# An attention kernel's start and end rearranged: loads in single blocks, statistics and paddings moved between engines, one key block in halves, another end of the exponential stream

## The chip, the cores and the metric

The kernel runs on one core of one Trainium2 chip. Its time is the device time of one execution in microseconds (us). The span in a profile, first to last instruction, is some 1.8 us shorter (867.1 in the profiled run of the kernel before, which took 868.85). Names of the engines: PE multiplies matrices (TensorE), PEld loads its weights, ACT is ScalarE, DVE is VectorE, POOL is GpSimd, SP issues DMA transfers. All runs gave correct results.

Ratios are the mean time of one kernel's fast runs over the mean of the other's fast runs of the same rounds on the same chip. So a ratio is not quite the ratio of the medians quoted beside it.

## The reference, cut to what matters

```
xn = layernorm(x)                                  # x: 2048 x 640
qkv = xn @ wqkv                                    # 32 heads of 20 columns
scores = einsum("bhqd,bhkd->bhqk", q, k) * 20**-0.5
p = softmax(scores);  o = einsum("bhqk,bhkd->bhqd", p, v);  s = o @ wo
g = silu(B(xn))        # a second branch: layernorm, two products over 2048 and 1536, gelu
out = x + s * g
```

The exponentials of the softmax are the bulk: 32 x 2048 x 2048 of them. ACT takes most in pieces of 128x1024 scores ("doubles", two banks of PSUM); DVE computes the rest with an integer formula in units of 128x512, so two DVE units equal one ACT double. They sum to 2,048 halves, for instance 888 doubles, one single and 271 units.

## The kernel before

The program is written by a builder in Python: a list scheduler with a model of durations decides the order of each engine's instructions. The parts that the change touches:

```python
    DMA_LAT = 1900.0                  # the scheduler's model of a load
    DMA_RATE = 300.0
    ACT_STATS = (1, 5)                # blocks of x whose mean and variance ScalarE computes
    DVE_TAIL_GUARD = 3                # DVE takes no unit among the last 3 of a pass
    # ... (cut)
        dma_x(0, 1)                   # block, number of blocks in one transfer
        dma_x(1, 1)
        dma_x(2, 1)
        dma_x(3, 1)
        dma_w(640, 736, wqk3[:, :, 640:736], S_("wk0"))      # first head group's weights
        dma_w(0, 96, wqk3[:, :, 0:96], S_("wq0"))
        dma_x(4, 4)
        dma_w(1280, 1440, wv_sb[:, :, 0:160], S_("wv0"))
        dma_x(8, 4)
        dma_x(12, 4)
    # ... (cut)
        add_job("wp0", [wp_step("dve", 1, 0, 250.0), wp_step("dve", 0, 0, 250.0), ("tag", "wpG0")], ("ln_s0",), 20.5)
    # ... (cut: the emission of one exponential on ScalarE)
            tk = pr.act(lambda e: e.activation(outp, inp, AF.Exp, ...),
                        reads=[bank_slot[b] for b in banks[:n]], writes=[...], name=f"exp{us[0]}", cost=...)
    # ... (cut: which unit DVE takes next)
            u = nxt[0]
            if u < NU and u + len(dg) > pass_end[u] - self.DVE_TAIL_GUARD:
                u = pass_end[u]
    # ... (cut: the last two output blocks; BA holds 512 columns, BB 128)
        BA, BB = (5, 0), (4, 1)
        def tail_fin(i):
            b = LBS[i]
            steps = op_mms(b, ps(BA[i]), 0, 512, bank_slot[BA[i]], False, True)
            steps += op_mms(b, ps(BB[i], 128), 512, 128, bank_slot[BB[i]], False, True)
```

Keys come in four blocks of 512 rows. A block of keys needs four 128-row blocks of x: statistics, normalization (DVE, with one POOL step), transposes (PE), an eviction, the projection (PE), another eviction.

The softmax here doesn't subtract the row's maximum and nothing guards it: scores larger than these inputs give would overflow.

Of the kernel before, what the change touches and what calls it, by code (L numbers as in the profile page):

```python
# [87 lines left out]
class Prog:  # L88
# [7 lines left out]
    DMA_LAT = 1900.0  # L96
    DMA_RATE = 300.0
# [185 lines left out]
class _Kern:  # L283
# [20 lines left out]
    ACT_STATS = (1, 5)  # L304
    H_PRIO = 88.0
    DVE_EXP = True
    DVE_TAIL_GUARD = 3
    NTMP = 4
# [90 lines left out]
    def schedule(self):  # L399
# [79 lines left out]
        dma_x(3, 1)  # L479
        dma_w(640, 736, wqk3[:, :, 640:736], S_("wk0"))  # L480
        dma_w(0, 96, wqk3[:, :, 0:96], S_("wq0"))
        dma_x(4, 4)
# [72 lines left out]
        def stat_steps(gb):  # L555
            steps = []
            b0 = gb * 4
            nm = f"ln{gb}"
            for b in range(b0, b0 + 4):
# [11 lines left out]
            steps.append(("tag", f"ln_s{gb}"))  # L571
            return steps

        def ln_steps(gb):
            steps = []
            b0 = gb * 4
            nm = f"ln{gb}"
            mvs = [S_(f"mv{b}") for b in range(b0, b0 + 4)]
            sr = S_(f"rstd{gb}")
            sw = S_(f"lnw{gb}")  # L580
            steps.append(("dve", lambda e: e.tensor_scalar(st(4, b0, 4), st(1, b0, 4), self.EPS, None, ALU.add), mvs,
                          [sw], f"{nm}ve", 100.0))
            steps.append(("pool", lambda e: e.tensor_tensor(st(2, b0, 4), st(4, b0, 4), mhalf(4), ALU.pow),
                          [sw, S_("mhalf")], [sr], f"{nm}pow", 1050.0))
            for b in range(b0, b0 + 4):
                steps.append(("dve", lambda e, b=b: e.tensor_scalar(xn_ap(b), regA[:, b, :], st_sb[:, 0, b:b + 1],
                                                                    st_sb[:, 2, b:b + 1], mean_op(b), ALU.mult),
                              [S_(f"x{b}"), mvs[b - b0], sr], [S_(f"xn{b % FC}")], f"{nm}ap", 360.0))
                steps.append(("tag", f"xn_b{b}"))
            steps.append(("tag", f"xn_g{gb}"))  # L590
            return steps

        def hstat_steps():

            mvs = [S_(f"mv{b}") for b in range(NB)]
            rs = [S_(f"rstd{gb}") for gb in range(4)]
# [22 lines left out]
        def wp_step(eng, w, G0, cost):  # L619
            dstp = bass.AP(wqk0_sb, w * 128, [[5 * 256, P], [256, 5], [32, GH], [1, 32]])  # L620
            srcp = bass.AP(wqk_sb, w * 640, [[6400, P], [1280, 5], [20, GH], [1, 32]])
            return (eng, lambda e: e.tensor_copy(dstp, srcp), [S_("wk0" if w else "wq0")], [S_(f"wp{w}_{G0}")],
                    f"wp{w}_{G0}", cost)
# [21 lines left out]
        def xT0_steps(half, dcs, nm):  # L645

            def make(bk):
                steps = []
                pb = ps_all[:, bk * 512:(bk + 1) * 512].bitcast(bf)
                for b in (2 * half, 2 * half + 1):  # L650
                    for i, dc in enumerate(dcs):
# [3 lines left out]
                            [S_(f"xn{b}"), S_("idb")], [bank_slot[bk]], "xT0", 128))  # L655
                n = len(dcs)
                dst = xnT_sb[:, dcs[0]:dcs[0] + n, half * 256:(half + 1) * 256]
                src = pb[:, 0:n * 256].rearrange("p (c n) -> p c n", c=n)
                steps.append(("ev", dst, src, "copy", None, [bank_slot[bk]], [S_(f"xT{dc}_0{half}") for dc in dcs],
                              "xTe0", n * 256))  # L660
                steps.append(("tag", f"xT0_{nm}"))
# [3 lines left out]
        def xsl(dc, tb, half=None):  # L665

            if tb:
                return [S_(f"xT{dc}_{tb}")]
            return [S_(f"xT{dc}_0{h_}") for h_ in ((0, 1) if half is None else (half,))]

        def qk0_steps(w, c0, n, half, nm):

            def make(bk):
                steps = []
                rd = [S_(f"wp{w}_0")] + [x for dc in range(5) for x in xsl(dc, 0, half)]
                for dc in range(5):
                    steps.append(("pe", lambda e, dc=dc: e.matmul(
                        ps(bk, n), wqk0_sb[:, dc, w, :], xnT_sb[:, dc, c0:c0 + n], start=(dc == 0),
                        stop=(dc == 4)), rd, [bank_slot[bk]], f"qk0_{w}_0{nm}", n))
                steps.append(("ev", qk_sb[:, 0, w, c0:c0 + n], ps(bk, n), "k" if w else "q", None,  # L680
                              [bank_slot[bk], S_("cq")], [S_(f"qkb0_{w}_0_{g}{nm}") for g in range(GH)], f"qke0_{w}_0{nm}", n))
                steps.append(("tag", f"qk0_{w}_0{nm}"))
# [3 lines left out]
        def qk_slots(slot, w, tb, g):  # L686
            if slot == 0 and tb == 0:
                return [S_(f"qkb0_{w}_0_{g}a"), S_(f"qkb0_{w}_0_{g}b")]
# [52 lines left out]
        def v_steps(b, half):  # L741
            def make(bk):
# [3 lines left out]
                for i, bb in enumerate(bl):  # L746
                    rd = [S_("wv0" if half == 0 else "wv")] + [x for dc in range(5) for x in xsl(dc, bb // 4, None if bb > 3 else bb // 2)]
# [328 lines left out]
        def unit_ok(u):  # L1076
            G, p, c, g = units[u]
            if G == 0 and c == 0 and p == 0:
                return "qk0_1_0a" in done and "qk0_0_0" in done
            return all(f"qk{G}_1_{x[0] // 4}" in done for x in parts[u]) and f"qk{G}_0_{p}" in done  # L1080

        def emit_st(lst, banks):
# [8 lines left out]
            for j2, (k2, i) in enumerate(rows_):  # L1091
# [11 lines left out]
                      reads=qk_slots(slot, 0, p, g) + (qk_slots(slot, 1, c // 4, g) if slot or c // 4 else  # L1103
                                                      [S_(f"qkb0_1_0_{g}" + ("a" if c == 0 else "b"))]), writes=[bank_slot[bk]],
# [192 lines left out]
        XT0 = ("a", "b", "c", "d", "e")  # L1297
        add_job("consts2", lambda bk: cst2 + [("tag", "qpad")], ("xn_g3",), 60.0)
        for gb in range(4):
            add_job(f"stat{gb}", stat_steps(gb), () if gb == 0 else (f"ln_s{gb - 1}",), 20.8 + gb)  # L1300
            rq = (f"ln_s{gb}",) + (() if gb < 3 else tuple(f"xT0_{d}" for d in XT0))
            add_job(f"ln{gb}", ln_steps(gb), rq, 20.0 + gb)
        for b in self.ACT_STATS:
            add_job(f"astat{b}", act_stats(b), (), 21.0 + b)
        add_job("wp0", [wp_step("dve", 1, 0, 250.0), wp_step("dve", 0, 0, 250.0), ("tag", "wpG0")], ("ln_s0",),
                20.5)
# [9 lines left out]
        def xts(b):  # L1316
            if b < 4:
                return tuple(f"xT0_{d}" for d in XT0)
            return tuple(f"xT{b // 4}_{d}" for d in (0, 2, 4))

        for nm, half, dcs in (("a", 0, (0, 1, 2, 3)), ("b", 0, (4,)), ("c", 1, (0, 1)), ("d", 1, (2, 3)), ("e", 1, (4,))):
            add_bank_job(f"xT0_{nm}", xT0_steps(half, dcs, nm), (f"xn_b{2 * half + 1}",), 22.0)
# [463 lines left out]
```

## Time and profile before

| | before |
|---|---|
| time, median of 3 runs | 870.96 us (868.67 to 871.2) |
| profiled run: time, span | 868.85 us, 867.1 us |
| first exponential starts | 15.16 |
| 27th exponential starts | 46.64 |
| last exponential ends (called E below) | 856.40 |
| end of the span | E + 10.70 |

The prediction shows the page's first lines, four stretches and the two timelines. Two more rows of the table of stretches cut the run at the 27th exponential (columns: stretch, length, busy us of PE, PEld, DVE, ACT, POOL with the number of instructions, clock, DMA share, GB/s):

```profile
15.16:46.64 31.48, 29.32 (x250) 15.26 (x253) 27.34 (x76) 27.61 (x32) 7.11 (x8) 1.00 0.34 81
46.64:856.40 809.76, 754.36 (x5470) 234.81 (x5555) 775.20 (x1911) 808.64 (x878) 0.00 (x0) 1.00 0.18 39
```

In the second row ACT is busy 808.64 of 809.76 us. The first one is the ramp. The chain that ended last shows the end of the run (start, length, engine and line):

```profile
859.41 0.33 PE ps_all L1216 x4
859.74 2.20 PE ps_all L873 x11
861.94 0.34 PE ps_all L878
```

L1216 are the last products of probabilities and values, L873 the eleven output products, L878 the closing ones that need the last rows of attention. DVE's epilogue makes these rows ready: it divides by the sums of the softmax and transposes, into a buffer called the stage.

### The profile page before, as it was taken

To read this page: it belongs to the slowest core of one execution; us is meant where nothing else is said; L and a number is where in the kernel's file an instruction comes from. 1 tells how busy PE (TensorE), PEld (TensorE's weight loads), DVE (VectorE), ACT (ScalarE), POOL (GpSimd) and SP (SyncE) were. 2 spreads that over 40 slices of the span, in tenths; PEclk is the share of its full clock that TensorE was granted. 3 is DMA by queue.
4 is the path that set the end of the run, shared out by engine and by line. 5 is a ranking of instruction groups with operands and counts; after the bars stand their busy time and mean duration, and the time that the engine had idled before them with its cause. 6 is when DMAs were issued, how large, how long until landed. Compare 5 with 4: busy or idle time off the path is not lost.

```text
span 867.1 us, 16589 instructions
## 1 busy us (share of the span) xinstructions
PE 801.2 (92%) x5837; PEld 260.4 (30%) x5928; DVE 820.6 (95%) x2040; ACT 844.8 (97%) x925; POOL 13.8 (2%) x22
## 2 busy tenths in 40 slices
PE   8999999999999999999899999999999999999997
PEld 4432222222232233322222322322222222222233
DVE  8989999999999999999999999999999999999998
ACT  6899999999999999999999999999999999999995
POOL 3200000000000000000000000000000000000000
PEclk9999999999999999999999999999999999999999
DMA  8141010011203113100013112122312200032120
GB/s 240 44 112 31 6 37 10 16 30 35 58 13 76 38 18 82 54 11 10 10 25 77 38 36 52 26 52 65 72 26 50 47 11 6 8 106 65 42 47 32
DMA packets 123303, 39.33 MB, mean 45 GB/s; under 512 B 84264, under 2 KB 122104, under 8 KB 123224
## 3 DMA queue, kind: packets, MB, share of 16 engines
q1 hardware_dynamic: 123224, 38.27, 18.9%
q8 instruction: 50, 0.82, 0.4%
q14 instruction: 29, 0.24, 0.1%
HBM read 25.88 MB, written 9.83 MB: 41 GB/s over the span
## 4 chain that ended last, share of the span: by engine, by line
ACT 82%; PE 10%; DVE 6%; issue 1%; DMA 1%; SPq 0%; DVEq 0%; ACTq 0%
ACT pt_sb L1129 80%; PE ps_all L1101 4%; DVE ew_sb L1169 1%; PE ps_all L1216 1%; DVE dpt_sb L1175 1%; PE ps_all L749 1%; ACT zt_sb L837 1%; DVE el_sb L1173 1%; PE ps_all L873 1%; DVE el_sb L1174 1%; DMA regA<-in_A_x_dram 1%; ACT zt_sb L832 1%; PE ps_all L804 1%; PE ps_all L697 1%; DVE el_sb L1171 0%
## 5 line engine op out<-in xcount | busy, mean ns | idle before, releaser
L1129 ACT ACTIVATE pt_sb<-ps_all 128x1024 bf16<-128x1024 f32 x889 | 820.3, 1136 | 3.1 <-PE ps_all L1101 2.1
L1101 PE MATMUL ps_all<-qk_sb 32*128 32x512 bf16 (+1 forms) x2112 | 367.5, 377 | 51.1 <-ACT pt_sb L1129 41.2
L1169 DVE TENSOR_SCALAR ew_sb<-ps_all 128x512 uint16<-128x512 uint16 x271 | 182.8, 685 | 26.9 <-PE ps_all L1101 25.2
L1101 PEld LDWEIGHTS ps_all<-qk_sb 32*128 32x128 bf16 x2112 | 97.6, 91 | 345.6 <-ACT pt_sb L1129 298.2
L1175 DVE SCALAR_TENSOR_TENSOR dpt_sb<-ps_all,el_sb 128x512 uint16<-128x512 f32 x271 | 179.7, 684 | 1.4
L1216 PE MATMUL ps_all<-pt_sb,v_sb 128*32 128x512 bf16 (+1 forms) x1832 | 162.7, 378 | 0.3 <-DVE dpt_sb L1175 0.3
L1173 DVE TENSOR_TENSOR el_sb<-ev_sb,el_sb 128x512 bf16<-128x512 bf16 x271 | 109.2, 417 | 0.5
L1174 DVE TENSOR_TENSOR el_sb<-el_sb,ew_sb 128x512 bf16<-128x512 bf16 x271 | 108.7, 418 | 0.4
L1216 PE MATMUL ps_all<-dpt_sb,v_sb 128*32 128x512 bf16 (+1 forms) x280 | 81.7, 378 | 0.3 <-DVE dpt_sb L1175 0.3
L804 PE MATMUL ps_all<-regB,regA 128*128 128x128 bf16 (+1 forms) x371 | 75.8, 300 | 1.4 <-issue 0.8
L1170 DVE TENSOR_SCALAR ev_sb<-ew_sb 128x512 bf16<-128x512 uint16 x271 | 74.1, 286 | 2.2
L804 PE MATMUL ps_all<-regC,regA 128*128 128x128 bf16 (+1 forms) x371 | 73.2, 300 | 1.3 <-issue 0.8
L1171 DVE TENSOR_SCALAR el_sb<-ew_sb 128x512 bf16<-128x512 uint16 x271 | 74.0, 285 | 0.0
L716 PE MATMUL ps_all<-xnT_sb,wqk_sb 128*112 128x512 bf16 x200 | 66.4, 403 | 0.3 <-DVE el_sb L1174 0.2
L1216 PEld LDWEIGHTS ps_all<-pt_sb,v_sb 128*32 128x32 bf16 x1832 | 36.0, 94 | 55.6 <-issue 49.0
L1682 PE MATMUL ps_all<-wrm_sb 128*128 128x512 bf16 (+1 forms) x145 | 44.8, 392 | 3.8 <-DVE ps_all L508 2.2
L804 PEld LDWEIGHTS ps_all<-regB,regA 128*128 128x128 bf16 x384 | 25.3, 97 | 40.1 <-issue 25.9
L804 PEld LDWEIGHTS ps_all<-regC,regA 128*128 128x128 bf16 x384 | 25.3, 97 | 38.5 <-issue 29.8
L749 PE MATMUL ps_all<-wv_sb,xnT_sb 128*128 128x160 bf16 (+1 forms) x160 | 33.7, 302 | 0.1
L873 PE MATMUL ps_all<-wo_sb,xnT_sb 128*128 128x128 bf16 (+2 forms) x154 | 30.9, 300 | 0.5 <-issue 0.3
L716 PEld LDWEIGHTS ps_all<-xnT_sb,wqk_sb 128*112 128x112 bf16 x200 | 21.4, 128 | 29.6 <-issue 10.8
L1690 PE MATMUL ps_all<-wrm_sb,v_sb 128*128 128x512 bf16 x80 | 28.4, 385 | 0.5 <-DVE rden_sb L1272 0.2
(89 smaller groups left out, 354.1 us busy)
## 6 DMA issues: line engine op xcount, KB each, us to landing
regA<-in_B_w_dram SPq DMA_DIRECT2D x6, 1024.0 KB
regA<-in_B_w_dram SPq DMA_DIRECT2D x8, 768.0 KB
regA<-in_A_x_dram SPq DMA_DIRECT2D x7, 640.0 KB
qkT_scratch_dram<-pk_sb SPq DMA_DIRECT2D x40, 112.0 KB
qk_sb<-qkT_scratch_dram SPq DMA_DIRECT2D x56, 80.0 KB
on_scratch_dram<-on_sb SPq DMA_DIRECT2D x124, 20.0 KB
out_dram<-regC SPq DMA_DIRECT2D x3, 640.0 KB
wqk_sb<-in_A_wqkv_dram SPq DMA_DIRECT2D x2, 680.0 KB
```

The source lines that it names most:

```text
L716: steps.append(("pe", lambda e, dc=dc: e.matmul(ps_all[0:112, bk * 512:(bk + 1) * 512], wqk_sb[:, dc * 1280 + c0:dc * 1280 + c0 + 112], xn ...
L804: steps.append(("pe", lambda e, k=k: e.matmul(ps(bk, n), wap[:, k, col0:col0 + 128], rows[:, k, c0:c0 + n], start=(k == 0), stop=(k == nk ...
L1101: pr.pe(lambda e, outp=outp, lhsT=lhsT, rhs=rhs, g=g: e.matmul(outp, lhsT, rhs, start=True, stop=True, tile_position=(32 * g, 0)), reads=q ...
L1129: tk = pr.act(lambda e: e.activation(outp, inp, AF.Exp, bias=-self.OFFS * math.log(2.0) / 128.0, scale=math.log(2.0) / 128.0), reads=[bank ...
L1169: (lambda e: e.tensor_scalar(w3, lo, 0x7FFF, None, ALU.bitwise_and), bs, [sw], dv(N)),
L1170: (lambda e: e.tensor_scalar(v_, w_, 1.0 / 256.0, -128.0, ALU.mult, ALU.add), [sw], [sv], dv(N, .26)),
L1171: (lambda e: e.tensor_scalar(l_, w_, a3 / 65536.0, (b3 - 64.0 * a3) / 256.0, ALU.mult, ALU.add), [sw], [sl_], dv(N, .26)),
L1173: (lambda e: e.tensor_tensor(l_, v_, l_, ALU.mult), [sv, sl_], [sl_], dv(N, .52)),
L1174: (lambda e: e.tensor_tensor(l_, l_, w_, ALU.mult), [sl_, sw], [sl_], dv(N, .52)),
L1175: (lambda e: e.scalar_tensor_tensor(o_, zr, -(self.OFFS - 16256.0), l_, ALU.add, ALU.add), bs + [sl_], [S_(f"dpt{s0 + i}") for i in range( ...
L1216: pr.pe(lambda e, outp=outp, lhsT=lhsT, rhs=rhs, k=k, g=g: e.matmul(outp, lhsT, rhs, start=(k == 0), stop=(k == NB - 1), tile_position=(0, ...
L1682: pe_full(lambda e: e.matmul(ps(wb, n), wrm_sb[:, 0:P], wrm_sb[:, P:P + n], start=True, stop=True), [S_("warm"), S_("warm1")], [bank_slot[ ...
```

## The change

The intent: start the exponentials earlier, close the hole in ACT's stream at key block 1, and shorten the end. The diff, cut to its core:

```diff
-    DMA_LAT = 1900.0
-    DMA_RATE = 300.0
+    DMA_LAT = 2000.0
+    DMA_RATE = 220.0
-    ACT_STATS = (1, 5)
+    ACT_STATS = (1,)
+    LN_GROUPS = ((0, 4), (4, 2), (6, 2), (8, 4), (12, 4))     # normalization: blocks 4-5 and 6-7 in pairs
+    LAST_GUARD = 10
@@ loads
+        dma_x(4, 1)
         dma_w(640, 736, ...)
         dma_w(0, 96, ...)
-        dma_x(4, 4)
+        for b in range(5, 8):
+            dma_x(b, 1)
@@ padding of the first head group's weights
-        add_job("wp0", [wp_step("dve", 1, 0, 250.0), wp_step("dve", 0, 0, 250.0), ...], ("ln_s0",), 20.5)
+        add_job("wp0", [wp_step(w) for w in (1, 0)] + [("tag", "wpG0")], (), 50.5)      # now on ScalarE
@@ key block 1 in halves
+            if gb == 1:
+                for nm, half, dcs in (("a", 0, (0, 1)), ("b", 0, (2, 3, 4)), ("c", 1, (0, 1)), ("d", 1, (2, 3)), ("e", 1, (4,))):
+                    add_bank_job(f"xT1_{nm}", xT0_steps(1, half, dcs, nm), ...)
+                    if nm == "b":
+                        add_bank_job("k0_1a", qk0_steps(1, 1, 0, 256, 0, "a"), ...)
+                add_bank_job("k0_1b", qk0_steps(1, 1, 256, 256, 1, "b"), ...)
@@ priority of probability-value products: later while the ramp lasts
-                    pr_ = 1.0 if nav >= self.PV_HI else (8.0 if ... else 70.0)
+                    pr_ = 1.0 if nav >= self.PV_HI else 30.0 if ramp[0] else (8.0 if ... else 70.0)
@@ the end
-        BA, BB = (5, 0), (4, 1)
+        BA, BB = (5, 7), (4, 0)
-            if u < NU and u + len(dg) > pass_end[u] - self.DVE_TAIL_GUARD:
+            if u < NU and u + len(dg) > pass_end[u] - (self.DVE_TAIL_GUARD if pass_end[u] < NU else self.LAST_GUARD):
+            if e == "dve" and nxt[0] >= NU:          # after the last unit, prefer DVE work of high priority that is ready soon
+                soon = [max(x[1], pr.T[e]) for x in cs_by[e] if x[0] <= 12.0]
+                if soon and min(soon) <= r + 130.0:
+                    r = min(soon)
```

## The prediction

> **What bounds the kernel now.** I read the page first (shares, forty slices, chain), then the timeline of ScalarE (ACT) at both ends, then the busy time of every engine in four stretches, then the waits.
>
> ```profile
> PE 801.2 (92%) x5837; PEld 260.4 (30%) x5928; DVE 820.6 (95%) x2040; ACT 844.8 (97%) x925; POOL 13.8 (2%) x22
> ...
> ACT 82%; PE 10%; DVE 6%; issue 1%; DMA 1%; SPq 0%; DVEq 0%; ACTq 0%
> ...
> L1129 ACT ACTIVATE pt_sb<-ps_all 128x1024 bf16<-128x1024 f32 x889 | 820.3, 1136 | 3.1 <-PE ps_all L1101 2.1
> ```
>
> ACT carries the end: 889 exponentials, with 3.1 us of idle in front of them in the whole run. Four stretches (columns: stretch, its length, then busy us of PE, PEld, DVE, ACT, POOL, clock, DMA share, GB/s) show where it is not busy:
>
> ```profile
> 0.00:15.16 15.16, 11.45 (x76) 7.70 (x76) 11.32 (x39) 7.50 (x15) 6.71 (x14) 1.00 0.90 277
> 15.16:44.81 29.65, 27.49 (x232) 14.29 (x234) 27.34 (x76) 25.79 (x29) 7.11 (x8) 1.00 0.30 68
> 44.81:856.40 811.59, 756.19 (x5488) 235.77 (x5573) 775.20 (x1911) 810.47 (x879) 0.00 (x0) 1.00 0.18 40
> 856.40:867.10 10.70, 6.03 (x50) 2.67 (x48) 6.76 (x17) 1.04 (x4) 0.00 (x0) 0.90 0.18 62
> ```
>
> So 811.6 us of 867.1 are a stream that ACT keeps full. Only the 15.2 us before the first exponential, the holes in the next 29.7 us, and the 10.7 us after the last one can shrink. ACT's timeline there:
>
> ```profile
> 9.81 0.74 ACT L549 ACTIVATE regC<-regA 128x640 bf16<-128x640 bf16 x1 [4.29 <-DMA regA<-in_A_x_dram]
> 10.45 0.19 ACT L549 ACTIVATION_READ_ACCUMULATOR regC<-regA 128x1 f32 x1
> 10.54 1.49 ACT L1023 ACTIVATE xnT_sb<-ps_all 128x1024 bf16<-128x1024 bf16 x2
> ...
> 15.16 7.72 ACT L1129 ACTIVATE pt_sb<-ps_all 128x1024 bf16<-128x1024 f32 x8
> 22.76 1.03 ACT L1023 ACTIVATE xnT_sb<-ps_all 128x1024 bf16<-128x1024 bf16 x1
> 25.22 0.78 ACT L1030 ACTIVATE qk_sb<-ps_all,cst_sb 128x512 bf16<-128x512 f32 x1 [1.42 <-PE ps_all L697]
> 26.48 3.90 ACT L1129 ACTIVATE pt_sb<-ps_all 128x1024 bf16<-128x1024 f32 x4 [0.48 <-PE ps_all L1101]
> ```
>
> The reader is to see two things. ACT waits until 9.81 for an x block that only feeds statistics, and the first transposed-x eviction stands behind it until 10.54. After eight exponentials (key block 0) the stream stops from 22.76 to 26.48 for key block 1: 3.7 us. Two smaller holes follow, 34.30 to 35.83 (key block 2) and 44.03 to 44.81 (key block 3), with one value eviction of 0.77 between.
>
> **What the Trainium skill says.** "TensorE: Matmul & The Clock Gate", Architectural detail, calls the ACT and DVE queues strict FIFO: an instruction that waits holds up those behind it. The trace agrees: the eviction at 10.54 waited behind the load. "ScalarE: Activation LUTs", What ACT_TABLE_LOAD costs, gives 186 ns + 0.833 ns per column for a plain activation, 719 ns for 640 columns; the trace has 737 ns for 128x640. That is my price for a weight padding on ACT. "DMA: Bandwidth & Descriptors", Specifications, puts the minimum for line rate at 512 B; the first weight loads have rows of 192 B, and the trace shows 162 GB/s from 5 to 6 us against 294 from 2 to 3 us. "Perfetto Trace Analysis", Engine Utilization, says at least one engine should approach full use in a well-tuned kernel; ACT at 97% does.
>
> **The change part by part.** Times are of the trace before; the order of instructions is that of the built program.
>
> *To the first exponential.* Statistics of block 5 leave ACT for DVE, so ACT no longer waits until 9.81. The two paddings leave DVE (0.30 and 0.35 us) for ACT, 0.74 each, in a gap of ACT that runs from 5.5 to about 9.8. The weights are now one 160 KB block later: they were there by 6.89 and 7.17; at 294 GB/s a block is 0.56 us, so by about 7.5 and 7.7, and the paddings end by 9.0 at worst. DVE now runs one half of block 4's statistics (0.36) ahead of the variance step, in place of one padding (0.22): x-normalization starts at 8.55 instead of 8.41. Block 4 should have landed: 820 KB are moved by 4.95, and block 2's semaphore came 1.2 us after its bytes, giving 6.2, before 6.89. The transposes of blocks 0 and 1 were done at about 9.75 before, so 9.9 now; the eviction starts then and not at 10.54. PE followed 1.15 us after it (11.69), so 11.05 now, and the rest of the chain is the same 2.9 us of projections and a last eviction. First exponential 15.16 - 0.6 = 14.55. **Gain 0.6 us.**
>
> *Key block 1.* Its blocks are normalized in pairs and transposed in halves, DVE takes these evictions. In the new order ACT runs 11 exponentials, one value eviction, 5 more: all 16 of key blocks 0 and 1 with no hole. Exponential 9 needs the first half by about 21.3; DVE, walked row by row, has it at 19.5. Exponential 13 needs the second by 25.1; DVE has it at 24.3, little room. The hole of 3.7 us closes.
>
> *What is given back.* DVE gets some 1.1 us of extra copies, 1.1 of key evictions and 1.1 of statistics, and loses 0.65 of padding and 0.96 of first evictions. Blocks 8 to 11 are normalized by about 28.2 instead of 26.15. Exponential 16 ends at 14.55 + 16*0.965 + 0.57 = 30.6. Then ACT has query block 1 (0.78), a transposed-x piece (0.57), a wait for five 512-column matmuls (1.24), key block 2 (0.78) and 0.5 for the score matmuls: exponential 17 at 34.5, 35.83 before. Key block 3's eviction also moves to ACT: 0.78 + 0.5 instead of 0.78 in all, and one value eviction follows (0.5). Exponential 25 at 43.5 (44.81 before), exponential 26 at 44.9 (45.75 before). **Of 3.7 us some 0.9 stay, the first part's 0.6 included.**
>
> *Middle.* 888 double exponentials in both; the last single one (707 ns) becomes a 272nd DVE unit. **Gain 0.5 us** at the spacing of the stream.
>
> *Tail.* Let E be the end of the last exponential, 856.40 before. The chain before, in DVE's timeline:
>
> ```profile
> 856.99 1.28 DVE L1175 SCALAR_TENSOR_TENSOR dpt_sb<-ps_all,el_sb 128x512 uint16<-128x512 f32 x2
> ...
> 859.78 0.45 DVE L1253 STREAM_TRANSPOSE tr_sb<-ps_all 128x256 f32<-128x256 f32 x1 [0.22 <-PE ps_all L1216]
> 860.26 0.20 DVE L1256 RECIPROCAL rden_sb<-tr_sb 128x8 f32<-128x8 f32 x1
> 860.50 0.33 DVE L1257 TENSOR_TENSOR on_sb<-tr_sb,rden_sb 128x160 bf16<-128x160 f32 x1
> 860.87 0.45 DVE L1258 STREAM_TRANSPOSE stage_sb<-on_sb 128x256 bf16<-128x256 bf16 x1
> 862.30 0.69 DVE L1455 TENSOR_TENSOR regC<-ps_all,regC 128x512 bf16<-128x512 f32 x1 [0.99 <-PE ps_all L878]
> ```
>
> DVE's last units end at E+1.9, the epilogue starts at E+3.4, its stage is ready at E+4.9, the last DVE operation ends at 864.58 = E+8.2, the output lands 2.5 later: E+10.7. With the guard of 10 units the last five exponentials leave DVE free: its last unit ends about E-2.6. The last probability-value matmuls wait for PE's five 512-column output matmuls and start at E+0.3, the epilogue at E+0.9, the stage is ready at E+2.4. But the second last block now takes bank 7, which three earlier jobs use in turn, so PE has 22 matmuls of 128 columns (0.1 each, to E+2.8), the first closing matmuls, then five of 512 columns (1.2) *behind* the stage, and two closing ones: E+4.8. ACT's evictions (0.8) and the last two DVE operations (1.0) follow, E+6.7, and the output at E+9.2. **Gain 1.5 us**, where the epilogue alone is 2.5 earlier.
>
> Sum: 0.9 + 0.5 + 1.5 = 2.9 us, 0.33%. From the median 870.96: 868.0.
>
> **The rivals.** (1) *The whole ramp gain stays*: if DVE is faster than my walk and key block 2 is ready when exponential 16 ends, 2 us more, 866. Against: four evictions on ACT in one place, and PE's order puts the transposes behind score matmuls. (2) *A new head-of-line wait takes the gain back*: ACT for the later weights, or DVE for block 4. The loads saturate the queues (DMA share 0.90 until 15 us); weights later than 9.8 would cost as much as the wait removed: 869 to 870. (3) *The DVE is the bound of the stream and the guard moves work the wrong way*: DVE is busy 95%, but it sat 25.2 us idle for score matmuls (L1169's row), so it has room; ACT's 3.1 us against it. (4) *The tail is bound by PE rather than by exponentials*: then only part of the 1.5 comes, 869. If bank 7 comes free sooner than I think, up to 1.5 more.
>
> **Range and chances.** Each part may be wrong by 1 to 1.5 us; three runs before spread from 868.67 to 871.2. In 8 of 10 cases 865.0 to 870.4. Two per cent would be 17.4 us, over half of the 33 us that are not full stream (15.2 + 10.7 + 7.3, the last being 29.65 less 24 exponentials of 0.93), so "within 2%" is nearly sure.
>
> **What would show it.** ACT: no wait for x after 4 us, two paddings before 9.1, first exponential at 14.3 to 14.8, sixteen with one eviction among them, then a hole of 3.5 to 4 us before the seventeenth near 34.5. Stretch from exponential 26 on: still no idle. Tail: last DVE unit before E, epilogue at E+0.9, span end at E+9.2, with five 512-column matmuls after the first closing ones. Wrong if padding waits, if the hole stays above 5 us, if ACT idles in the middle, or if the tail is still over 10 us.

## The result, and the profile after

The changed kernel took 867.0 us in the median of 6 runs (866.84 to 868.73), the kernel before 870.73 beside it (868.67 to 872.5, 6 runs). All outputs are right. The ratio is 0.9962, 95% interval 0.9946 to 0.9978: same within 2%, and 1 us under the predicted 868.0. In the profiles the span went from 867.1 to 865.0, 2.1 us. The other 1.6 us of the medians are taken up under e9. The parts below are differences of two single profiles: in the five profiles whose order is that of the changed kernel up to 850 us (after, e1, e6, e8, e9) the first exponential starts at 14.12 to 14.38 and the 28th at 47.01 to 47.30, so a part of 0.3 us is no more than this scatter.

The table of stretches of the changed kernel, cut at the same events (first exponential, 27th exponential, E):

```profile
0.00:14.38 14.38, 10.41 (x79) 7.11 (x79) 12.00 (x43) 8.38 (x15) 7.39 (x15) 1.00 0.81 241
14.38:46.19 31.81, 29.59 (x264) 16.04 (x264) 26.68 (x75) 28.12 (x34) 6.58 (x8) 1.00 0.37 90
46.19:855.38 809.19, 752.56 (x5450) 230.68 (x5537) 779.29 (x1917) 807.89 (x876) 0.00 (x0) 1.00 0.18 40
855.38:865.00 9.62, 5.04 (x41) 2.27 (x40) 5.62 (x13) 1.04 (x3) 0.00 (x0) 1.00 0.20 70
```

Row by row against before: the start is 0.78 us shorter (14.38 against 15.16), the ramp 0.33 longer (31.81 against 31.48), the stream 0.57 shorter (809.19 against 809.76), the tail 1.08 shorter (9.62 against 10.70). The sum is 2.10. ACT's timeline of the ramp shows where the 0.78 went:

```profile
6.67 1.51 ACT L628 ACTIVATE wqk_sb<-wqk_sb 128x640 bf16<-128x640 bf16 x2 [1.14 <-DMA wqk_sb<-in_A_wqkv_dram]
9.72 1.51 ACT L1029 ACTIVATE xnT_sb<-ps_all 128x1024 bf16<-128x1024 bf16 x2 [1.53 <-PE ps_all L658]
...
14.38 10.28 ACT L1137 ACTIVATE pt_sb<-ps_all 128x1024 bf16<-128x1024 f32 x11
24.61 0.57 ACT L1029 ACTIVATE v_sb<-ps_all 128x480 bf16<-128x480 f32 x1
25.08 1.93 ACT L1137 ACTIVATE pt_sb<-ps_all 128x1024 bf16<-128x1024 f32 x2
27.27 2.85 ACT L1137 ACTIVATE pt_sb<-ps_all 128x1024 bf16<-128x1024 f32 x3 [0.25 <-PE ps_all L1109]
30.00 0.79 ACT L1036 ACTIVATE qk_sb<-ps_all,cst_sb 128x512 bf16<-128x512 f32 x1
30.66 0.62 ACT L1029 ACTIVATE xnT_sb<-ps_all 128x512 bf16<-128x512 bf16 x1
32.62 0.78 ACT L1036 ACTIVATE qk_sb<-ps_all,cst_sb 128x512 bf16<-128x512 f32 x1 [1.35 <-PE ps_all L703]
33.88 5.71 ACT L1137 ACTIVATE pt_sb<-ps_all 128x1024 bf16<-128x1024 f32 x6 [0.48 <-PE ps_all L1109]
...
43.13 1.02 ACT L1137 ACTIVATE pt_sb<-ps_all 128x1024 bf16<-128x1024 f32 x1 [0.49 <-PE ps_all L1109]
44.05 0.57 ACT L1029 ACTIVATE v_sb<-ps_all 128x480 bf16<-128x480 f32 x1
44.51 1.03 ACT L1137 ACTIVATE pt_sb<-ps_all 128x1024 bf16<-128x1024 f32 x1
46.19 1.94 ACT L1137 ACTIVATE pt_sb<-ps_all 128x1024 bf16<-128x1024 f32 x2 [0.65 <-PE ps_all L1109]
```

The paddings sit in a gap of ACT and end by 8.2; the wait until 9.81 for x is gone. Sixteen exponentials run with one eviction among them. Then the work that had stood in the hole of key block 1 stands in one heap in front of the 17th: query block 1, a piece of transposed x, 1.35 us of waiting for PE, key block 2, another 0.48. The 17th starts at 33.88 where it had been 35.83, 1.95 earlier, and the 27th only 0.45 earlier: three quarters of the lead are lost at the evictions of key block 3 and values (41.87 to 44.51) and in a wait of 0.65 in front of the 27th.

At the end, DVE's timeline:

```profile
852.41 0.69 DVE L1183 SCALAR_TENSOR_TENSOR dpt_sb<-ps_all,el_sb 128x512 uint16<-128x512 f32 x1
855.65 0.69 DVE L893 TENSOR_TENSOR regC<-ps_all,regC 128x512 bf16<-128x512 f32 x1 [2.55 <-PE ps_all L884]
856.53 0.45 DVE L1261 STREAM_TRANSPOSE tr_sb<-ps_all 128x256 f32<-128x256 f32 x1 [0.19 <-PE ps_all L1224]
...
857.61 0.45 DVE L1266 STREAM_TRANSPOSE stage_sb<-on_sb 128x256 bf16<-128x256 bf16 x1
```

and the chain that ended last:

```profile
857.84 0.70 PE ps_all L879 x7
858.54 0.38 PE ps_all L884 x2
...
858.97 1.13 PE ps_all L879 x4
860.10 0.39 PE ps_all L884 x2
```

The stage is written last at 857.61. DVE's last unit ends at 853.10, before E, and the epilogue starts at E+1.15 where it had been E+3.38, 2.2 us earlier. The last closing product, however, ends at 860.48 = E+5.1, where it had been 862.59 = E+6.2: 1.1 earlier. PE still has output products to do (L879), here on either side of the first pair of closing ones (L884).

### The profile page after: what moved, and what is told of

It reads as the page before. It is cut to its first block, busy times and chain, and to the rows that moved or that the text cites. A ratio compares the mean times of both kernels' runs of the same rounds, so it can differ in the third digit from the quotient of the medians.

```text
span 865.0 us, 16498 instructions
## 1 busy us (share of the span) xinstructions
PE 797.6 (92%) x5828; PEld 256.1 (30%) x5918; DVE 823.6 (95%) x2047; ACT 845.4 (98%) x925; POOL 14.0 (2%) x23
## 4 chain that ended last, share of the span: by engine, by line
ACT 87%; PE 9%; DVE 2%; POOL 1%; issue 1%; ACTq 0%; POOLq 0%
ACT pt_sb L1137 85%; PE ps_all L1109 3%; PE ps_all L1224 1%; ACT zt_sb L843 1%; PE ps_all L755 1%; PE ps_all L879 1%; ACT zt_sb L838 1%; PE ps_all L1704 1%; DVE ew_sb L1177 0%; PE ps_all L683 0%; PE ps_all L722 0%; POOL v_sb L1298 0%; PE ps_all L703 0%; DVE dpt_sb L1183 0%; PE ps_all L658 0%
## 5 line engine op out<-in xcount | busy, mean ns | idle before, releaser
L1183 DVE SCALAR_TENSOR_TENSOR dpt_sb<-ps_all,el_sb 128x512 uint16<-128x512 f32 x272 | 182.0, 684 | 1.8
L1181 DVE TENSOR_TENSOR el_sb<-ev_sb,el_sb 128x512 bf16<-128x512 bf16 x272 | 111.0, 417 | 1.1
L1224 PE MATMUL ps_all<-dpt_sb,v_sb 128*32 128x512 bf16 (+1 forms) x279 | 83.7, 379 | 0.0
L722 PE MATMUL ps_all<-xnT_sb,wqk_sb 128*112 128x512 bf16 x200 | 68.2, 405 | 0.4 <-DVE zt_sb L816 0.4
L1696 PE MATMUL ps_all<-wrm_sb 128*128 128x512 bf16 (+1 forms) x117 | 34.0, 376 | 3.9 <-DVE ps_all L513 2.2
L1704 PE MATMUL ps_all<-wrm_sb,v_sb 128*128 128x512 bf16 x97 | 34.0, 385 | 1.3 <-issue 0.7
L879 PE MATMUL ps_all<-wo_sb,xnT_sb 128*128 128x128 bf16 (+3 forms) x151 | 30.2, 298 | 1.1 <-issue 0.5
```

Source lines behind the costliest of these rows:

```text
L722: steps.append(("pe", lambda e, dc=dc: e.matmul(ps_all[0:112, bk * 512:(bk + 1) * 512], wqk_sb[:, dc * 1280 + c0:dc * 1280 + c0 + 112], xn ...
L1181: (lambda e: e.tensor_tensor(l_, v_, l_, ALU.mult), [sv, sl_], [sl_], dv(N, .52)),
L1183: (lambda e: e.scalar_tensor_tensor(o_, zr, -(self.OFFS - 16256.0), l_, ALU.add, ALU.add), bs + [sl_], [S_(f"dpt{s0 + i}") for i in range( ...
L1224: pr.pe(lambda e, outp=outp, lhsT=lhsT, rhs=rhs, k=k, g=g: e.matmul(outp, lhsT, rhs, start=(k == 0), stop=(k == NB - 1), tile_position=(0, ...
L1704: pe_full(lambda e: e.matmul(ps(AB), zero, wrm_sb[:, P:P + 512], start=new, stop=new), [S_("warm"), S_("v_ones")], [sl_acc], "warmz", 512)
```

## The experiments

The theory after the result: the start moved as predicted; three quarters of the ramp's lead are lost by the 27th exponential; the guard does not free DVE so much as it decides how much work PE has left at E. The rivals: the bank makes the tail, a single part of the ramp is responsible, or the clock explains the difference. All runs are of 5 rounds, beside runs of the kernel before.

One table first. Start of the 1st and 28th exponential; pace, which is E minus the 28th's start over the number of doubles from there (a single counts half); E; tail (span end minus E); PE busy within the tail; span of the profiled run; and, from all runs, the median time of those with a mean clock of 0.998 or more (their number). The columns but the last come from one profile each. The profiles of e3, e7 and e9 have a stretch of 3.41 us at half clock in the middle (at 585, 686 and 625 us), and that of e4 has one from 11.65 to 15.07. In e9, whose order is that of the changed kernel, it moved E by 0.6 us; ACT waited 1.00 us for scores in e3's and 0.95 in e7's. About 0.001 of the paces of e3 and e7 is such waiting.

| kernel | 1st | 28th | pace | E | tail | PE in tail | span | time at clock 0.998 and above |
|---|---|---|---|---|---|---|---|---|
| before | 15.16 | 47.57 | 0.9389 | 856.41 | 10.70 | 6.02 | 867.1 | 868.3 to 868.7, by batch (19) |
| after | 14.38 | 47.12 | 0.9387 | 855.38 | 9.62 | 5.04 | 865.0 | 866.97 (5) |
| e1 ramp only | 14.38 | 47.13 | 0.9386 | 854.80 | 10.70 | 6.20 | 865.5 | 867.36 (5) |
| e2 tail only | 15.06 | 47.39 | 0.9401 | 858.26 | 9.44 | 5.09 | 867.7 | 869.42 (3) |
| e3 query block 1 later | 14.33 | 46.98 | 0.9419 | 858.47 | 9.43 | 5.32 | 867.9 | 868.71 (5) |
| e4 old priority | 16.09 | 49.02 | 0.9406 | 859.85 | 9.25 | 5.10 | 869.1 | 869.37 (5) |
| e5 statistics only | 14.01 | 47.23 | 0.9428 | 859.43 | 9.67 | 5.35 | 869.1 | 871.21 (5) |
| e6 old banks | 14.12 | 47.01 | 0.9387 | 855.20 | 9.60 | 5.11 | 864.8 | 866.93 (4) |
| e7 paddings on DVE | 14.34 | 46.41 | 0.9442 | 859.33 | 9.27 | 5.16 | 868.6 | 869.54 (2) |
| e8 guard 6 | 14.33 | 47.30 | 0.9386 | 854.99 | 10.71 | 6.21 | 865.7 | 867.50 (5) |
| e9 after again | 14.25 | 47.14 | 0.9394 | 855.99 | 9.61 | 5.05 | 865.6 | 867.27 (5) |
| e10 weights first | 13.76 | 47.60 | 0.9410 | 858.72 | 9.28 | 5.01 | 868.0 | 870.43 (6) |
| e11 model numbers | 14.58 | 46.11 | 0.9407 | 856.96 | 8.34 | 4.02 | 865.3 | 867.36 (4) |
| e12 statistics, other order | 14.37 | 47.54 | 0.9406 | 857.84 | 10.36 | 5.91 | 868.2 | 870.44 (3) |

### e1: the ramp without the new tail

```diff
 (against the changed kernel)
-    LAST_GUARD = 10
+    LAST_GUARD = 3
-        BA, BB = (5, 7), (4, 0)
+        BA, BB = (5, 0), (4, 1)
 (and the rule "soon" taken out)
```

> The changed kernel with its tail undone: guard of 3 units, old tail banks, no waiting rule on DVE; the ramp is instruction for instruction that of the changed kernel. Theory (ramp worth 0.5 us at the stream's start, rest from the balance of units and the tail): exponential 1 at 14.4, exponential 27 at 46.2, DVE 273 units, last exponential ends at 854.9, tail again 10.7, span 865.6, ratio to before 0.998. Rival A (the ramp's gain is wholly given back before exponential 27, only the tail pays): span 867, ratio 1.000. Rival B (the ramp carries all): ratio 0.996.

Measured: 867.36 us (867.05 to 867.39), ratio 0.9947 (0.9924 to 0.9970). The 1st exponential is at 14.38 as in the changed kernel. Without the guard E is 0.58 us earlier (854.80) and the tail 1.08 longer (10.70). So the tail part is worth the difference, 0.5 us of span (865.5 against 865.0), not the 1.1 by which the tail alone shrank. The ramp with an unchanged tail is 1.6 us of the 2.1. But only 0.45 of these are there at the 28th exponential; 0.94 is one double less on ACT (887 and one single, against 888 and one), since this order gives DVE 273 units and not 271, as the theory had it. The ratio is below the expected 0.998 because seven of the eleven runs of the kernel before had clocks of 0.993 to 0.995; at 0.998 and above the medians are 867.36 and 868.64 (3 runs), 1.3 us.

### e2: the tail without the new ramp

```diff
 (against the kernel before)
+    LAST_GUARD = 10
-        BA, BB = (5, 0), (4, 1)
+        BA, BB = (5, 7), (4, 0)
 (and LAST_GUARD at the two places where the guard is read, and the rule "soon")
```

> The kernel before with the new tail alone: guard of 10, banks 5,7 and 4,0, waiting rule on DVE; ramp as before. DVE gets 269 units (271 before), ACT one double exponential more. Theory: last exponential ends 0.9 later, at 857.3, tail 9.6 instead of 10.7, span 866.9, ratio 0.9995 to 1.000: the guard alone pays almost nothing. Rival A (the tail pays all): span 865.0, ratio 0.996. First exponential 15.16 under both.

Measured: 870.13 us (869.32 to 872.27), ratio 0.9985 (0.9959 to 1.0010), which does not tell it from the kernel before; the few runs at a clock of 0.998 and above are 0.8 us slower (869.42, 3 runs, against 868.64, 3 runs). The tail shrank as it did in the changed kernel (10.70 to 9.44), E came 1.85 us later: half of it because two DVE units fewer leave one double more to ACT (0.94), the rest waits for scores in the middle (0.92 us at one place, 821.66). So of the 1.26 us that the guard takes from the tail, 0.94 are given back by the units. The other 0.92 are not shown to be the guard's. ACT's instructions come in the same order as before up to 855 us, and PE's weight loads up to 852, but here an output product stood for a DMA transfer at the head of PE's queue, with the scores behind it (the same product in the kernel before, then here):

```profile
819.49 0.39 PE L873 MATMUL ps_all<-wo_sb,xnT_sb 128*128 128x512 bf16 x1
820.91 0.39 PE L874 MATMUL ps_all<-wo_sb,xnT_sb 128*128 128x512 bf16 x1 [1.56 <-DMA xnT_sb<-on_scratch_dram]
```

The transfer was issued at 816.61 (816.12 before). Without the wait the span would be about 866.8, and the theory had 866.9. Whether the other runs had it too is not recorded.

### e6: the old banks

```diff
 (against the changed kernel; only the last PE products change their order)
-        BA, BB = (5, 7), (4, 0)
+        BA, BB = (5, 0), (4, 1)
```

> The changed kernel with the old banks (5,0) and (4,1) for the last two output blocks; only the order of PE's last 18 matmuls differs, everything before is the same. Both theories: first exponential 14.38, E about 855.4. Theory: the banks are worth little: block 15 starts four of its five 512-column matmuls before the closing ones, while the epilogue of VectorE runs anyway, so the tail is 9.2 to 9.7 us (9.62 in the changed kernel), ratio to the kernel before as the changed kernel's at equal clock, span 864.6 to 865.1. Rival: bank 7 is what shortened the tail from 10.70: then 10.2 or more, span 865.6 or more.

Measured: 866.95 us (866.72 to 868.52), ratio 0.9982 (0.9970 to 0.9994), tail 9.60 against 9.62. The rival falls: the banks are worth nothing. The ratio is nearer to 1 than the changed kernel's only because the kernel before ran better in this batch (868.47).

### e8: a guard of 6

```diff
-    LAST_GUARD = 10
+    LAST_GUARD = 6
```

> The changed kernel with the last guard at 6 units instead of 10 (3 before): VectorE takes one exponential more (273) and ScalarE half an exponential less or the same (887 and one single). Theory: the guard only trades the time of the last exponential against the length of the tail: E at 854.8 to 855.1 (855.38 in the changed kernel, 854.80 with guard 3 and the old banks), tail 9.6 to 10.3, span 864.6 to 865.4, that is the changed kernel's 865.0 within 0.4. Rival: a guard of 10 frees VectorE more than is needed, and with 6 the tail stays at 9.6 while E gains 0.5: span 864.4 or less, the fastest of all.

Measured: 867.5 us (867.29 to 867.55), ratio 0.9984 (0.9972 to 0.9996). E is 854.99, the tail 10.71 and the span 865.7, a little above the range for tail and span. The rival (a tail that stays at 9.6) falls: a guard of 6 has the tail of a guard of 3. DVE's epilogue is hardly later, since the stage that PE's closing products read was written from 857.75 where it was 857.61 in the changed kernel (0.5 us more when counted from E); PE has 6.21 us of work left at E and not 5.04.

Over all fourteen profiles the tail less PE's busy time in it lies between 4.1 and 4.7 us, while the tail itself goes from 8.34 to 10.71. In none of them does PE idle more than 0.16 us between E and its last product, and the end comes 4.1 to 4.5 us after that product. So the tail follows what PE has left to do at E. It holds at the short end too: e11, with the same guard, banks and rule as the changed kernel, has 30 products left instead of 41:

```profile
856.96:865.30 8.34, 4.02 (x30) 1.52 (x28) 4.76 (x12) 1.04 (x4) 0.00 (x0) 0.91 0.22 79
```

### e3: query block 1 later

```diff
-            add_bank_job(f"q0_{p}", ..., 64.0 * p - 44.0, 64.0 * p)
+            add_bank_job(f"q0_{p}", ..., 64.0 * p - (24.0 if p == 1 else 44.0), 64.0 * p)
```

> The changed kernel with query block 1 released 20 units later, so its eviction no longer stands on ACT between exponential 16 and key block 2. Theory (the hole before exponential 17 is made of ACT's own evictions and the wait for key block 2): ACT has 1.03 + 0.78 there instead of 0.79 + 0.62 + 0.78, exponential 17 starts at 33.4 instead of 33.88; no value eviction after exponential 25, so exponential 27 is 0.8 to 1.2 earlier than 46.19; with one single exponential more, last exponential ends 0.5 earlier, ratio 0.9956. Rival (hole set by when blocks 8 to 11 are normalized, DVE): exponential 17 stays at 33.9.

Measured: 868.71 us (868.43 to 870.09), ratio 0.9969. Taking query block 1 out of the heap did not bring the 17th exponential forward: 33.92 against 33.88. ACT then waits 1.42 us for PE's projection of key block 2 (1.35 in the changed kernel). The expectation failed, but the run does not free the hole of ACT's evictions, since one was exchanged for another: without query block 1, ACT evicts a whole piece of transposed x there,

```profile
30.18 1.06 ACT L1029 ACTIVATE xnT_sb<-ps_all 128x1024 bf16<-128x1024 bf16 x1
```

to 31.24, where the changed kernel evicts query block 1 and half a piece, to 31.28. PE's projection of key block 2 waits for this eviction in both (0.21 and 0.62 us). The rival's cause is not the limit either: DVE has blocks 8 to 11 normalized by 27.1 (27.3 in the changed kernel). So the chain is an eviction by ACT, then PE's projection; which of the two a change should shorten, e3 does not tell.

### e4: the old priority of probability-value products

```diff
-                    pr_ = 1.0 if nav >= self.PV_HI else 30.0 if ramp[0] else (8.0 if ... else 70.0)
+                    pr_ = 1.0 if nav >= self.PV_HI else (8.0 if ... else 70.0)
```

> The changed kernel with the old priority of probability-value matmuls in the ramp (8 instead of 30). Theory (the lower priority mainly orders PE and is worth little): exponential 17 within 0.7 us of 33.9, ratio 0.996 within 0.001. Rival (that priority is what lets key block 1 be ready in time): a hole over 1 us inside the first sixteen exponentials, ratio 0.998 or more.

Measured: 869.37 us (869.09 to 870.96), ratio 0.9974. The profiled run is the slowest of the five: from 10 to 15 us PE's granted clock was 0.67, and the first exponential came at 16.09. The other four, at a clock of 1.000, had spans of 867.3 to 867.7, still some 2.5 us over the 864.9 to 865.4 of the changed kernel at such clocks. Waits of 0.28, 1.32 and 1.44 us stand in the ramp (at the 11th exponential, at key block 2, in front of the 25th). The 17th comes at 36.20, 20.1 us after the first where the changed kernel has 19.5, so the ramp alone loses little, and the hole of the rival is not there. The old priority makes the kernel 2.4 us slower, but the total mixes it with the pace of another order (0.9406), so its own worth stays open.

### e5: only the statistics of block 5

```diff
 (against the kernel before)
-    ACT_STATS = (1, 5)
+    ACT_STATS = (1,)
```

> The kernel before with one part of the change: the statistics of block 5 move from ScalarE to VectorE, nothing else. Theory: the first exponential comes 0.6 to 0.8 us earlier, at 14.4 to 14.6 (15.16 before), because ScalarE no longer waits until 9.81 for block 5; but the exponential after the hole of key block 1 is set by VectorE's normalization of blocks 4 to 7, which now carries 1.1 us more statistics, and not by the start of the stream, so it comes no earlier than before (26.48 before; 26.0 to 27.5 here). The hole grows by what the start gained, E (end of the last exponential, 856.40 before) stays at 856.0 to 857.5, ratio 1.000 +- 0.001. Rival: the 0.7 us carry through to the end: the exponential after the hole at 25.8, E at 855.7, ratio 0.9992 or less at equal clock.

Measured: 871.29 us (870.97 to 874.01), ratio 1.0035 (1.0022 to 1.0048): slower than the kernel before by a third of a per cent, clear of the noise. Neither theory had it. ACT's timeline:

```profile
14.01 7.52 ACT L1129 ACTIVATE pt_sb<-ps_all 128x1024 bf16<-128x1024 f32 x8
21.41 1.03 ACT L1023 ACTIVATE xnT_sb<-ps_all 128x1024 bf16<-128x1024 bf16 x1
23.87 0.78 ACT L1030 ACTIVATE qk_sb<-ps_all,cst_sb 128x512 bf16<-128x512 f32 x1 [1.42 <-PE ps_all L697]
25.13 7.67 ACT L1129 ACTIVATE pt_sb<-ps_all 128x1024 bf16<-128x1024 f32 x8 [0.48 <-PE ps_all L1101]
33.85 1.94 ACT L1129 ACTIVATE pt_sb<-ps_all 128x1024 bf16<-128x1024 f32 x2 [1.05 <-PE ps_all L1101]
```

The hole of key block 1 is still there (21.41 to 25.13), and yet the 9th exponential starts 1.35 us earlier than before (26.48) and the 17th at 33.85, where the whole change has 33.88. My theory, that DVE's load would eat the gain at the 9th, was wrong. So up to the 17th this one line has the whole lead. At the 28th the leads are small in all of them: 47.23 here, 47.54 in e12 (the same ramp, with x in place 0.36 us later), 47.12 to 47.14 in the changed kernel, 47.57 before. It is after the 28th that 3 us are lost. ACT's waits for scores, summed over the run, are 5.0 us in 12 places in e5 and 3.0 in 7 in the changed kernel; before 48 us they are alike.

### e7: the paddings back on DVE

```diff
 (against the changed kernel)
-            return ("act", lambda e: e.activation(dstp, srcp, AF.Copy), ...)
+            return ("dve", lambda e: e.tensor_copy(dstp, srcp), ...)
-        add_job("wp0", [...], (), 50.5)
+        add_job("wp0", [...], ("ln_s0",), 20.5)      # after the statistics of blocks 0 to 3
```

> The changed kernel with the two weight paddings back on VectorE, behind the statistics of blocks 0 to 3 as before. Theory: the move to ScalarE pays nothing at the start, since ScalarE had a gap and VectorE's two copies are 0.22 and 0.35 us: first exponential 14.4 to 14.8 (14.38 in the changed kernel), E within 0.7 us of 855.4, span within 0.8 us of 865.0. The built order has one value eviction less on ScalarE after exponential 25, which may give back 0.5. Rival: the paddings held VectorE's normalization: first exponential at 15.0 or later and span 865.6 or more.

Measured: 871.0 us (869.34 to 874.66), ratio 1.0027 (1.0011 to 1.0044). At the start the theory holds: 14.34, so the move to ScalarE is worth nothing there. The 28th exponential even comes at 46.41, 0.7 earlier than in the changed kernel, with 2.25 us of evictions on ACT between the first and the 28th and not 4.11 (query block 1 and key block 3 are not among them). The total fits neither: the theory's span was 865.0 within 0.8, and the rival's span of 865.6 or more came without its late start. E is 859.33, at the worst pace of all, 0.9442 (about 0.943 without the stretch of half clock); the two runs at a clock of 0.999 and above took 869.34 and 869.74, still some 2.5 us more than the changed kernel.

### e10: the weights ahead of block 4

```diff
-        dma_x(4, 1)
         dma_w(640, 736, ...)
         dma_w(0, 96, ...)
-        for b in range(5, 8):
+        for b in range(4, 8):
             dma_x(b, 1)
```

> The changed kernel with the first weights ahead of block 4 again (x still in single blocks, all else as in the changed kernel). Theory: the place of block 4 in the queue is worth nothing at the start: ScalarE pads in a gap that lasts until 9.7, so weights 0.5 us earlier end in the same wait, first exponential 14.1 to 14.5 (14.38, 14.12 and 14.33 in three profiles of the changed ramp). What it moves is the order that the scheduler builds, so the end is not told by the start: waits of ScalarE after 48 us between 0.4 and 2.8 as in the runs so far, span 864.8 to 868.5. Rival: block 4 behind the weights holds up VectorE's variance step, and the first exponential comes at 14.8 or later.

Measured: 870.43 us (869.88 to 870.89), ratio 1.0002 (0.9966 to 1.0038). The first exponential comes at 13.76, earlier than in every other kernel: the built order puts the variance step of DVE at 6.34 us instead of 7.12, since it no longer has block 4's statistics in front. So the fifth block ahead of the weights, for itself, costs 0.4 to 0.6 at the start; the rival falls the other way round than it was put. And again it pays nothing: at the 28th exponential this kernel is the last but one (47.60). The ratio near 1 hides a slower kernel, since two runs of the kernel before had low clocks (see e9): at 0.998 and above it is 870.43 against 868.71, 1.7 us slower.

### e11 and e12: other numbers in the scheduler's model, the same parts

```diff
 (e11, against the changed kernel)          (e12, against e5)
-    DMA_LAT = 2000.0                       -    DMA_RATE = 300.0
-    DMA_RATE = 220.0                       +    DMA_RATE = 260.0
+    DMA_LAT = 1900.0
+    DMA_RATE = 300.0
```

> The changed kernel with the old numbers of the builder's load model (1900 ns, 300 GB/s in place of 2000 and 220): no instruction is added or removed in kind, but the list scheduler orders nearly all of them anew. Theory: these two numbers are not neutral; the first exponential stays at 14.1 to 14.5, but the order of the ramp and the middle changes, so that waits of ScalarE for score matmuls after 48 us are 1 to 3 us (0.63 in the changed kernel) and the span is 866 to 869. Rival: the order matters little once the stream is full: middle waits 0.4 to 0.7, span 864.6 to 865.6.

> The kernel of e5 (statistics of block 5 on VectorE, 869.1 us of span, waits of 2.78 us after 48 us) with 260 in place of 300 in the load model. The built order is the same in the first 1,040 rows of PE, that is over 40% of the run, and another after that. Theory: e5 lost its ramp gain only through the order of the middle; so the ramp is the same here (first exponential 14.0 to 14.3, the 25th at 43.9 to 44.2, waits between 48 and 300 us about 1.0 as in e5), and the later waits, 1.8 us in e5, come out different by 0.5 us or more, the span with them: anything from 866.5 to 870. Rival: the statistics on VectorE cost 3 us in the middle by themselves, whatever the order: the same 1.8 us of later waits within 0.3 and a span of 868.8 to 869.5.

Measured: e11 867.69 us (867.08 to 868.86 in five runs of clock 0.997 and above, one of 878.96 at 0.984), ratio 0.9993 (0.9942 to 1.0044, widened by that one run and two such of the kernel before); at a clock of 0.999 and above 867.08 to 868.01, against 866.9 to 867.29 of the changed kernel in e9. The theory had the waits (1.4 us after 48 us) but not the span. e12 871.12 us (870.18 to 872.12), ratio 1.0010 (0.9974 to 1.0047), but at a clock of 0.998 and above 870.44 against 868.71 of the kernel before.

e12 is the cleanest test of the pace. It has the instructions of e5 but for a few of PE's filler products, which only keep PE busy (269, where e5 has 270), and ACT's come in the same order up to 413 us. E came 1.6 us earlier (857.84 against 859.43); the later waits of ACT were 0.59 us and not 1.8, as the theory had it. So of the 3 us that e5 lost before E, about half is the order in which the scheduler set the same work (its tail was 0.7 longer, so that the spans differ by 0.9). The rest, a pace of 0.9406 against 0.9389, is not accounted for; another order might have it or not.

e11 shows the same for the changed kernel: its order leads at the 28th exponential (46.11) by a whole microsecond and has the shortest tail (8.34), loses 1.6 us in between (862 doubles at 0.9407 instead of 0.9388), and ends within half a microsecond of the changed kernel.

### e9: the changed kernel again, for the clock

No edit.

> The changed kernel once more, unaltered, beside runs of the kernel before on the same chip, to split the difference of the medians (870.73 against 867.0) into schedule and clock. Theory: the schedule is worth 1.2 to 2.1 us at equal clock (runs of the kernel before at a mean granted clock of 0.998 or more were 868.0 to 868.64, those of the changed kernel 866.84 to 867.14), and the rest of 3.7 us came from more runs of the kernel before with a clock of 0.993 to 0.997. So at equal clock 866.7 to 867.2 against 868.0 to 868.7, ratio 0.9975 to 0.9985 if the chip holds its clock. Rival: the whole 3.7 us belong to the kernel: ratio 0.996 again, also among runs of clock 0.998 and above.

Measured: 867.28 us (866.9 to 867.5, 6 runs), the kernel before 868.72 beside it (868.31 to 878.47, 11 runs), ratio 0.9965 with a wide interval (0.9925 to 1.0004), because two of the runs before had clocks of 0.992 and 0.983 and took 874.77 and 878.47. Among runs with a mean clock of 0.998 or more, the medians are 868.71 (9 runs) and 867.27 (5 runs): 1.44 us. In the first result such a split gives 866.84 to 867.14 for five of the six runs after. So the 3.7 us of the first medians are about 1.4 us of schedule at equal clock, 2.1 between the two profiled runs (the profile of before, 867.1, is at the upper end of the 866.2 to 867.2 of its runs at clock 0.998 and above in e5 to e12), and the rest is that more of the runs before had a lower mean clock. Over the three batches of experiments its clock was under 0.998 in 14 of its 33 runs. In the five kernels with the changed kernel's order of the middle (after, e1, e6, e8, e9) it was so in 3 of 27. Whether the order causes that, no run settles.

For the first result this split is carried over and not measured, since the clocks of its runs of the kernel before are not on record.

No version beat the changed kernel. e6 is equal to the changed kernel within its spread, e1, e8 and e11 are 0.1 to 0.5 us behind at equal clock.

## Why the prediction was right or wrong

The number was right, 868.0 against 867.0 and inside the range, and so was "within 2%". Its sum was 2.9 us, of which the profiles show 2.1 and the runs at equal clock 1.4. It came out near the first result, which had 3.7, most likely because the median that it started from, 870.96, held lower clocks (they are not on record; one of those three runs was 868.67). That nearness is in part luck. By its steps:

1. *First exponential at 14.55.* Right: 14.38, 14.25 in e9, 14.12 to 14.38 in kernels with the same ramp. The eviction started at 9.72 where it said 9.9. Its argument held as well (a wait for data that nobody needs yet, ahead of one that all need): e5 with that wait alone removed has the gain. The paddings fitted the gap of ACT (6.67 to 8.18) and ScalarE's price for one was the 0.74 us that it used (the 719 ns beside it are an estimate by the page's formula). One of its readings is weak: the 162 GB/s that it lays to rows of 192 B are those of 5 to 6 us, with 392 such packets; from 4 to 5 us, with 869 of them, the same trace has 237. Nothing else in the sum rests on it.
2. *Key block 1: no hole, sixteen exponentials with one eviction.* Right, with a wait of 0.25. But halving the block is not what won the ramp: e5 keeps the hole and has its 17th exponential at the same time.
3. *What is given back: the 17th at 34.5, the 25th at 43.5, the 26th at 44.9.* Right in kind, each put 0.4 to 0.6 too late: 33.88, 43.13, 44.51. **The step that failed is the sentence that some 0.9 of 3.7 us stay.** It stopped at the 26th exponential and took the stream to be full from there. The next one waited 0.65 us for its scores, and 0.45 remained. What the runs showed in its place: the lead is not handed on from one exponential to the next. Kernels whose first exponential differs by 0.8 us (13.76 to 14.58), all with the statistics moved (e4 with its half clock left out), stand between 46.1 and 47.6 at the 28th, in no order with their start. That PE was 93% busy there (29.59 of 31.81) speaks for PE as the limit of the ramp; I have not shown it by taking work off PE. A rival is ACT's own evictions: from the first to the 28th exponential they are 3.16 us before and 4.11 in the changed kernel, and the two kernels that lead at the 28th have the least (e7 2.25, e11 2.52). No run separates the two.
4. *Half an exponential less on ACT: 0.5.* Right: the stream from the 27th on is 0.57 shorter, at the same pace.
5. *Tail: E+9.2, 1.5 gained.* Right in mechanism, mis-sized: E+9.62, 1.08 gained. The stage was ready at E+2.7 (2.4 predicted), the products and last operations ended 0.2 to 0.3 later than added up. Bank 7, on which the order was blamed, made no difference (e6). And the gain of the tail was not the gain of the guard: e1 shows that the guard takes 0.6 of it back from E, so that the new tail as a whole is worth 0.5 us of span. Rival 4, the tail bound by PE, was the better sentence: the fourteen tails say so.
6. *Middle: no idle.* Right for the changed kernel (waits of 0.63 us in two places), and by no means a matter of course. Of the seven kernels whose order of the middle was set anew (e3, e4, e5, e7, e10, e11, e12), none kept a pace of 0.939. The five whose stream ran at full clock had 0.9406 to 0.9428, which over 862 doubles is 1.5 to 3.4 us, as much as the whole change or more. Not all of a pace is order: e2 had 0.9401 in the order of the kernel before, by the one late transfer. I had not counted that risk at all.

## What to carry to other kernels

When a list scheduler orders the program, an ablation by total time mostly measures a new order of the middle. Compare the same event in each kernel (the first, the 28th, the last exponential, the end) and read what each part does up to the next event. Before calling a difference order, see what ended the waits, and whether the clock held: one late transfer and one stretch of half clock were worth 0.9 and 0.6 us here in unchanged orders. At the end of a stream, look at what each engine has left when the bounding engine stops: moving work off one engine in the last microseconds pays only what it takes from the longest of the queues that remain, less what the stream itself lost.

## What the Trainium skill lacked or had wrong

- "TensorE: Matmul & The Clock Gate", What's actually happening: it describes the half-rate state of the array and says that the amount of slow work at the start of a kernel varies from run to run. The runs agree that it varies, and add a price and later places. In e4's profile a stretch of 3.41 us at half clock, from 11.65 us, went with a span of 869.1 us where the other four runs had 867.3 to 867.7. In e9's profile such a stretch at 625 us moved E by 0.6 us, where the first profile of the same program had none. On one chip the kernel before took 868.7 us at a mean clock of 0.998 or more and 874.8 at 0.992. The page has no word on comparing two medians under that.
- "Perfetto Trace Analysis", Identifying the Most-Contended Engine: it advises the engine with the highest occupancy. Here ACT, with 97%, set the stream, but the tail (8.34 to 10.71 us) followed PE's leftover work with a constant of 4.1 to 4.7 us. Under Optimization Strategy the same page allows that this engine changes over time, but it lacks a view of what is left in each queue when the busiest engine stops.
- No page that I read has the effect of instruction order alone: the same instructions but for a few fillers in another order had E at 857.84 and 859.43 (e12 and e5).
